# Attention and two expert blocks: the second block's table of rows kept in SBUF, and VectorE's operations in the attention in another order

## The chip, the core and the metric

The kernel runs on one NeuronCore of a Trainium2 chip. The core has TensorE (PE, matrix products), VectorE (DVE), ScalarE (ACT), GpSimd (POOL) and SyncE (SP, which here only issues transfers), and 16 DMA engines between DRAM and the on-chip memory SBUF; products land in the banks of PSUM. Each engine works through its own instructions in the order in which they are written. The metric is the device time of one execution in microseconds, and the numbers compared are medians of several runs.

## What is computed

Linear attention over 8 batches, 8 heads and 576 rows, then two blocks of experts over the 4608 rows with 8 experts each, of which every row uses one. The features of the attention are exponentials of a projection:

```python
def phi(x):
    proj = np.einsum('bhsd,df->bhsf', x, w_phi)
    proj = proj - np.max(np.abs(proj), axis=-1, keepdims=True)
    return np.concatenate([np.exp(proj), np.exp(-proj)], axis=-1)
q_p, k_p = (phi(q), phi(k))
kv = np.einsum('bhsf,bhsd->bhfd', k_p, v)
z = np.sum(k_p, axis=2)
num = np.einsum('bhsf,bhfd->bhsd', q_p, kv)
den = np.einsum('bhsf,bhf->bhs', q_p, z)[..., None] + 1e-06
return num / den

# a block: the expert of a row is the argmax of its logits
e_idx = np.argmax(logits, axis=1)
for e in range(E):
    mask = e_idx == e
    h = np.maximum(x[mask] @ w1[e], 0.0)
    out[mask] = gate_w[mask, None] * (h @ w2[e])   # block 2: also * sigmoid(x @ w_output_gate)[mask, e]
```

## The kernel before

**Products in halves.** Values in float32 are split into a high and a low float16 part, and three products stand for one (lines 878 to 880, 900 to 902). So every operand is scaled by a power of two and split first: `x_scale`, `x_hi` (ScalarE) and `x_lo` (VectorE) for the rows of the attention, `y_max`, `y_scale`, `y_hi`, `y_lo` for those of block 1.

**The attention** (to about 570 us) is a loop over steps t, nine for each batch, t = 9b + s. A step handles a pair of heads in several stages of a pipeline that lie some steps apart: projection of the keys and queries, then on VectorE the maxima `km` and `nm` and the difference `kd` (`k_max`, `q_max`, `k_sub`); five steps later the products `num` on TensorE, one more step later the division (`num_out` calls `norm`: `den`, its reciprocal, `xt`). A finished batch has its rows scaled and split (`x_hi` and `x_lo` at lag 16: 16 steps after the row's own), transposed on TensorE (`a_T`, lag 17, which reads both halves in the tile `rows_f`), and their logits are formed (`x_logits`, lag 18). In the steps with s = 1 the loop writes `a_T` ahead of `num`, in all others behind it.

**The splitter** (`Splitter.matrix`) prepares the weights of both blocks beside all this. For each expert and each of its two matrices (w = 0 and 1) it loads four quarters (`load`, two steps ahead), takes each quarter's largest magnitude (`mx`: on VectorE for w = 0; for w = 1 on ScalarE, whose line 247 writes `junk` and keeps the maximum), joins the four (`wm`, line 251, VectorE, and an all-reduce on GpSimd), and then forms `hi` on ScalarE and `lo` on VectorE and stores both to DRAM. Block 1's own steps do this for block 2's weights, in half-tile steps.

**The blocks.** A block goes through tiles of 128 rows, each of one expert: 40 main tiles and `E` = 3 more whose expert is found on the chip. Rows are gathered by an index (`gather`, an indirect DMA on GpSimd's queue), transposed (line 440 of `transposes`), and pass two products with a relu between (`first`, `hidden`, `second`); the relu's high half is written by ScalarE (line 889) and its low half by VectorE (line 890, tile `qs`). Rows that leave block 1 are scaled, split, transposed and given their logits of block 2; for each group of G = 4 tiles `gates` forms gates and one-hot choices, `gates_ranks` counts by products, `gates_store` stores the rows to `x2_d` and enters them in the table of block 2.

**The table.** Block 2 must know which stored row stands in which place of which expert. `places` works out a place for each of a group's rows. For the groups 0 to 8 of block 1, `enter` then writes the row's number (4 bytes) at that place: one indirect DMA (a scatter of 128 elements, line 434) for each of the group's four tiles, into four tables in DRAM that the attention had zeroed (`zeros`). The last group, and all of block 1's own table, go another way: `hots` writes two one-hot matrices for each tile on VectorE (lines 405 and 407, 128 x 128 with a code in place of the one, and 128 x 288), `tab_add` multiplies them in 12 products (line 416) into a bank of PSUM, and the result is added to a table of 96 x 384 in SBUF (`tab_out`), from which `tab_pick` reads by products and `decode` recovers the numbers. `route_a` and `route_b` form the indices of block 2 between the blocks: for block 2 from all four tables, read back from DRAM, and from the last group's.

The order of work on every engine is the order in which the functions are called. Short chains of VectorE operations are woven in by `Weave.step`, one operation at each `yield`.

```python
def enter(n, pi, c, r):
    nc.gpsimd.indirect_dma_start(
        out=tab_d[n][c][:, :], out_offset=bass.IndirectOffsetOnAxis(ap=pi[:, c : c + 1], axis=0),
        in_=row_no[n][:, r : r + 1], in_offset=None, bounds_check=NROW - 1, oob_is_err=False)
```

Of the kernel before, what the change touches and what calls it, by code (L numbers as in the profile page):

```python
# [26 lines left out]
DM = H * D  # L27
# [8 lines left out]
BIG = 8192.0  # L36
FAR = 65536.0
G = 4
# [16 lines left out]
def attention_two_moe(  # L55
# [15 lines left out]


    tab_d = [[dpool.tile([NROW, 1], F32, name=f"tab{n}_{k}") for k in range(K)] for n, K in enumerate((0, G))]
# [39 lines left out]
    row_no = [None]  # L113
    for n in (1,):
        nc_ = rows_of[n] // 128
        cn = const.tile([128, nc_], F32, name=f"cn{n}")
        nc.gpsimd.iota(cn, [[1, nc_]], base=-nc_, channel_multiplier=0, allow_small_or_imprecise_dtypes=True)
        t = const.tile([128, nc_, 2], F16, name=f"row_no{n}")
        nc.vector.tensor_copy(t[:, :, 0], cn)
        nc.vector.tensor_copy(t[:, :, 1], iota_p.to_broadcast([128, nc_]))  # L120
        row_no.append(t.rearrange("p c t -> p (c t)").bitcast(F32))


    tab0 = const.tile([96, 3, 128], F16, name="tab0")
    nc.gpsimd.memset(tab0, 0.0)
    code = const.tile([128, 5, 8], F32, name="code")
    nc.gpsimd.iota(code, [[0, 5], [-128, 8]], base=2047, channel_multiplier=-1, allow_small_or_imprecise_dtypes=True)
    for g in range(4):
        nc.vector.tensor_scalar(code[:, g], code[:, g], float(1 << (4 - g)), None, op0=ALU.mult)
    code = code.rearrange("p g c -> p (g c)")  # L130

    code1 = const.tile([128, G], F32, name="code1")
    nc.gpsimd.iota(
        code1, [[-128, G]], base=2047 - 128 * ((NMAIN - G) % 8), channel_multiplier=-1,
        allow_small_or_imprecise_dtypes=True)
    nc.vector.tensor_scalar(code1, code1, float(1 << (5 - (NMAIN - G) // 8)), None, op0=ALU.mult)
# [77 lines left out]
    class Splitter:  # L214
# [11 lines left out]
        def matrix(self, t0, e, w, stage):  # L226
# [12 lines left out]
            def mx(i):  # L239
# [9 lines left out]
                if i == 3:  # L249
                    m1 = self.sm.tile([128, 1], F32, tag="wm1", name="wm1")  # L250
                    nc.vector.tensor_reduce(out=m1, in_=st["mx"], op=ALU.max, axis=AX.X)
                    st["ma"] = self.sm.tile([128, 1], F32, tag="wma", name="wma")
                    nc.gpsimd.partition_all_reduce(st["ma"], m1, 128, RMAX)
# [113 lines left out]
    def places(ps, oh16, C, n, valid=None, chip=False):  # L367
# [19 lines left out]
        if n == 1 and not chip:  # L387
            return pi
# [10 lines left out]
    def hots(at_, pk, po, codes, mems):  # L399
# [3 lines left out]
        for c, m in enumerate(mems):  # L403
            a, o = m[:, 0:128], m[:, 128:416]
            nc.vector.tensor_scalar(
                a, iota128, pk[:, c : c + 1], codes[:, c : c + 1], op0=ALU.is_equal, op1=ALU.mult)
# [13 lines left out]
    def tab_out(ps):  # L420
        nc.vector.tensor_tensor(tab0, tab0, ps[0:96], op=ALU.add)

    def decode(out_, ps, tag, w, n=0):
# [4 lines left out]
        nc.vector.tensor_scalar(bits, bits, -1.0, float((137 << 10) + (5119, 6143)[n]), op0=ALU.mult, op1=ALU.add)  # L428
# [3 lines left out]

    def enter(n, pi, c, r):
        nc.gpsimd.indirect_dma_start(
            out=tab_d[n][c][:, :], out_offset=bass.IndirectOffsetOnAxis(ap=pi[:, c : c + 1], axis=0),
            in_=row_no[n][:, r : r + 1], in_offset=None, bounds_check=NROW - 1, oob_is_err=False)
# [68 lines left out]
    def zeros(z):  # L505

        nc.gpsimd.memset(z, 0.0)
        big = z[0:1, NROW // 128 :]
        nc.gpsimd.memset(big, BIG)
        yield  # L510
        for n in range(2):
            for t in tab_d[n]:
                nc.sync.dma_start(out=t.rearrange("(p c) o -> p (c o)", p=128), in_=z[:, 0 : NROW // 128])
                yield
        w = XW // 2
# [71 lines left out]
    etab = [None, const.tile([128, len(tab_d[1]), E], F32, name="etab1")]  # L587
# [38 lines left out]
    def early_rows(n):  # L626

        ereg[n] = [
            nc.values_load(eni[n][0:1, i : i + 1], engines=(ET.SP,), min_val=0, max_val=NE - 1) for i in range(2)]
        for k, t in enumerate(tab_d[n]):  # L630
            nc.sync.dma_start(
                out=etab[n][:, k],
                in_=t.rearrange("(e r) o -> e (r o)", e=NE)[ds(ereg[n][0], 1), 0 : E * 128].rearrange(
                    "e (c p) -> p (e c)", p=128))

    def early_sel():
# [4 lines left out]
            out=ec, in0=eno[0][:, 0:1].to_broadcast([128, E]), scalar=float(C1), in1=ec, op0=ALU.mult, op1=ALU.add)  # L641
# [6 lines left out]
    def tab_pick(ps, sel, tab=tab0):  # L648
        for k in range(3):
            nc.tensor.matmul(ps, tab[:, k], sel[:, k], start=(k == 0), stop=(k == 2))  # L650

    def early_idx(n, ps=None):
        if n == 0:
            yield from decode(eidx[0], ps, "ebits", E)
        else:
# [1330 lines left out]
```

## Time and profile before

| | before |
|---|---|
| Median of three runs | 1509.79 us (1503.33, 1509.79, 1510.79) |
| Profiled execution | 1502.37 us, its span 1500.5 us |
| Busy in the span: TensorE, VectorE, ScalarE, GpSimd | 1401.5, 824.6, 649.0, 198.7 us |
| Granted clock of TensorE, mean | 0.962 of full speed |
| DMA | 286.50 MB in 162224 packets, 191 GB/s in the mean |

The stages in the profiled execution: attention to about 521 us, its last rows and the turn to block 1 to 572, block 1 to 1064, the turn to block 2 to 1100, then block 2. Windows are stretches of the span; a row has each engine's busy time with the number of its instructions. In a timeline row stand the start, the duration in us, engine, line, operation, what it writes and reads, shapes, and in brackets the idle time ahead of it with what ended it; "issue" there means that the engine waited for nothing that the profile shows. In a row of waits stand the engine and line that waited, what released it, us in total, times, and the longest. The queue q8 carries instructions, q1 the transfers that SyncE issues, q0 those of GpSimd.

### The profile page before, as it was taken

The numbers are of one execution on the slowest core, as the hardware profiler recorded it, in microseconds if no ns is written. First come the engines' busy times: TensorE is split into PE (matmuls) and PEld (weight loads), VectorE is DVE, ScalarE is ACT, GpSimd is POOL, SyncE is SP. The second block draws the span as 40 slices with busy tenths as digits, with TensorE's granted clock in tenths as the row PEclk, the third lists the DMA queues.
The fourth block names the chain that finished last, engine by engine and source line by source line (L and its number), as shares of the span: only waits on it lengthen the run. The fifth ranks groups of instructions, "written<-read, shape, count | busy, mean of one in ns | idle before, by whom it ended". The sixth has DMA issues, their size and how long they took to land. (4 is left out here: it accounts for less than half of the span.)

```text
span 1500.5 us, 39967 instructions
## 1 busy us (share of the span) xinstructions
PE 1401.5 (93%) x16045; PEld 1134.8 (76%) x16045; DVE 824.6 (55%) x2469; ACT 649.0 (43%) x1010; POOL 198.7 (13%) x244
## 2 busy tenths in 40 slices
PE   6999999989989989999999789889999999999997
PEld 4998888988889877767777567667677777777764
DVE  3677887887887767667777467555621111111110
ACT  1457566766758432555556346443211111111111
POOL 1000000000000001212221121122022121121211
PEclk8999999999999889999999899999999999999998
DMA  8377858768663544578878788789835262773470
GB/s 242 112 208 233 257 169 259 217 233 249 201 199 114 210 191 130 191 191 226 220 218 258 147 181 242 157 229 358 241 110 155 72 191 65 240 229 93 130 239 30
DMA packets 162224, 286.50 MB, mean 191 GB/s; under 512 B 88537, under 2 KB 91117, under 8 KB 154864
## 3 DMA queue, kind: packets, MB, share of 16 engines
q1 hardware_dynamic: 146496, 242.29, 54.7%
q0 software_dynamic: 13504, 41.42, 8.5%
q8 instruction: 129, 2.11, 0.6%
q14 instruction: 63, 0.52, 0.1%
q10 hardware_dynamic: 2032, 0.16, 0.1%
HBM read 444.63 MB, written 99.24 MB: 362 GB/s over the span
## 5 line engine op out<-in xcount | busy, mean ns | idle before, releaser
L890 DVE SCALAR_TENSOR_TENSOR qs<-proj,qs 128x512 f16<-128x512 f32 x107 | 73.6, 688 | 270.8 <-ACT qs L889 270.8
L1497 PE MATMUL num<-kvsb,E 128*128 128x65 f32 x1024 | 128.4, 280 | 28.7 <-DVE xt L1481 27.0
L878 PE MATMUL proj<-xT,w 128*128 128x128 f16 x896 | 153.2, 220 | 1.3 <-DMA xT<-xg 0.7
L880 PE MATMUL proj<-xT,w 128*128 128x128 f16 x896 | 153.1, 220 | 0.1
L879 PE MATMUL proj<-xT,w 128*128 128x128 f16 x896 | 153.2, 220 | 0.0
L1497 PEld LDWEIGHTS num<-kvsb,E 128*128 128x128 f32 x1024 | 123.4, 197 | 33.5 <-issue 23.7
L880 PE MATMUL proj<-xT,v 128*128 128x128 f16 x816 | 140.5, 220 | 4.9 <-issue 4.9
L878 PE MATMUL proj<-xT,v 128*128 128x128 f16 x816 | 140.5, 220 | 0.0
L879 PE MATMUL proj<-xT,v 128*128 128x128 f16 x816 | 140.4, 220 | 0.0
L889 ACT ACTIVATE qs<-proj 128x512 f16<-128x512 f32 x107 | 63.5, 593 | 173.9 <-PE proj L880 142.9
L878 PEld LDWEIGHTS <-w 128*128 128x128 f16 x1344 | 132.3, 98 | 7.1 <-issue 5.0
L879 PEld LDWEIGHTS <-w 128*128 128x128 f16 x1344 | 132.3, 98 | 4.1 <-issue 2.1
L1412 PE MATMUL kv<-v,kp 128*128 128x128 f32 x1024 | 135.2, 288 | 0.0
L880 PEld LDWEIGHTS <-w 128*128 128x128 f16 x1344 | 132.3, 98 | 0.7 <-issue 0.6
L900 PE MATMUL num<-w,qs 128*128 128x512 f16 x336 | 127.3, 379 | 0.6 <-DMA w<-pl 0.6
L902 PE MATMUL num<-w,qs 128*128 128x512 f16 x336 | 127.3, 379 | 0.0
L901 PE MATMUL num<-w,qs 128*128 128x512 f16 x336 | 127.3, 379 | 0.0
L1412 PEld LDWEIGHTS kv<-v,kp 128*128 128x128 f32 x1024 | 126.4, 201 | 0.4 <-issue 0.4
L878 PEld LDWEIGHTS <-v 128*128 128x128 f16 x1216 | 120.0, 99 | 7.9 <-issue 5.7
L901 PE MATMUL num<-ks,qs 128*128 128x512 f16 x304 | 116.5, 383 | 9.2 <-issue 9.1
L902 PE MATMUL num<-ks,qs 128*128 128x512 f16 x304 | 116.6, 384 | 6.9 <-issue 6.9
L901 PEld LDWEIGHTS <-qs 128*128 128x128 f16 x640 | 62.9, 98 | 78.3 <-issue 13.1
(371 smaller groups left out, 3626.6 us busy)
## 6 DMA issues: line engine op xcount, KB each, us to landing
w<-pl SPq DMA_DIRECT2D x152, 1024.0 KB
v<-pl SPq DMA_DIRECT2D x80, 1024.0 KB
ks<-pl SPq DMA_DIRECT2D x80, 1024.0 KB
pl<-wo SPq DMA_DIRECT2D x66, 512.0 KB
w<-in_moe_w_dram SPq DMA_DIRECT2D x64, 512.0 KB
wf<-in_moe_w_dram SPq DMA_DIRECT2D x64, 512.0 KB
pl<-qs SPq DMA_DIRECT2D x26, 512.0 KB
ks<-in_k_dram SPq DMA_DIRECT2D x16, 576.0 KB
```

Of the source, the lines that this page charges most:

```text
L878: nc.tensor.matmul(h[:, j], wk[:, 0, cs], xT[:, k], start=(k == 0), stop=False)
L879: nc.tensor.matmul(h[:, j], wk[:, 0, cs], xT[:, 4 + k], start=False, stop=False)
L880: nc.tensor.matmul(h[:, j], wk[:, 1, cs], xT[:, k], start=False, stop=(k == 3))
L889: nc.scalar.activation(out=hi, in_=h, func=AF.Relu)
L890: nc.vector.scalar_tensor_tensor(out=lo, in0=h, scalar=0.0, in1=hi, op0=ALU.max, op1=ALU.subtract)
L900: nc.tensor.matmul(y, h[:, 0, k], wk[:, 0], start=(k == 0), stop=False)
L901: nc.tensor.matmul(y, h[:, 0, k], wk[:, 1], start=False, stop=False)
L902: nc.tensor.matmul(y, h[:, 1, k], wk[:, 0], start=False, stop=(k == 7))
L1412: nc.tensor.matmul(ps[:, half, h % 2], kp[:, c, half, :], vw(v1, 4 * h + c), start=(h % 2 == 0 and half == 0 and c == 0), stop=False)
L1497: nc.tensor.matmul(ps[:, c, 0:V], e[:, half, 128 * c : 128 * c + 128], kw(g, half), start=(half == 0), stop=(half == 1))
```

## The change

All ten groups of block 1 are entered by products into a second table in SBUF, `tabs[1]`. The scatters, their four tables in DRAM, the zeroing of these and both reads of them are gone; `hots` now runs for every group, and `enter_rows` issues the 12 products between `first` and `hidden` of the next tile. `early_idx` and `route_b` read the table by three products and `decode`, for both blocks alike.

In the attention three things change places. `norm` runs its first two operations (`den` and reciprocal) ahead of `k_max`, so that `xt` follows `km` directly and stands ahead of `nm`. `x_lo` has lag 17 instead of 16 and stands right behind the end of `norm`, so in the step of its row's `a_T`. In the splitter the maximum on ScalarE comes one step (in block 1 one half-tile step) earlier, while `wm` and the all-reduce, now in `most`, stay where they were.

```diff
@@ in Splitter.matrix
-                if i == 3:
-                    m1 = self.sm.tile([128, 1], F32, tag="wm1", name="wm1")
...
+                if i == 3 and w == 0:
+                    most()
+
+            def most():
+                m1 = self.sm.tile([128, 1], F32, tag="wm1", name="wm1")
...
-                job(u, "mx", mx, i)
+                job(u - w, "mx", mx, i)
...
+            if w == 1:
+                job(t0 + 3 * gap, "mx", most)
@@ the table
-    def tab_out(ps):
-        nc.vector.tensor_tensor(tab0, tab0, ps[0:96], op=ALU.add)
+    def tab_out(n, ps):
+        nc.vector.tensor_tensor(tabs[n], tabs[n], ps[0:96], op=ALU.add)
...
-    def enter(n, pi, c, r):
-        nc.gpsimd.indirect_dma_start(
...
@@ in early_rows and route_a: the reads of the tables in DRAM
-        for k, t in enumerate(tab_d[n]):
-            nc.sync.dma_start(
-                out=etab[n][:, k],
...
-            nc.sync.dma_start(out=tab, in_=t.rearrange("(k c p) o -> c k (p o)", k=3, p=128))
@@ in route_b
-            for x in range(2):
-                for i, t in enumerate(tab16):
-                    for k in range(3):
-                        nc.tensor.matmul(
-                            rows[:, x], t[:, k, :, x], sel[:, k], start=(i == 0 and k == 0),
-                            stop=(i == len(tab16) - 1 and k == 2))
-            last = state["pg"][:, 3, 2 * M : 3 * M]
-            tab_pick(last, sel, state["tab1"])
...
+        tab_pick(n, state["pg"][:, 3, 0:M], sel)
+        done(decode(idx, state["pg"][:, 3, 0:M], "bits", M, n))
@@ in gates_store
-        pi = yield from places(gate.pop((j, "rk")), gate.pop(j), g_, 1, val2[:, i0 : i0 + g_])
-        for c in range(g_):
-            enter(1, pi, c, i0 + c)
+        pk, po = yield from places(gate.pop((j, "rk")), gate.pop(j), g_, 1, val2[:, i0 : i0 + g_])
+        at_ = []
+        yield from hots(
+            at_, pk, po, codes[1][:, i0:],
+            [state["late"].tile([128, 416], F16, tag="hot", name="hot", bufs=G) for _ in range(g_)])
+        state["hots"] = at_[0]
...
+    def enter_rows():
+
+        if "hots" in state:
+            state["pts"] += 1
+            tab_out(1, tab_add(state["pt"][state["pts"] % len(state["pt"])], state.pop("hots")))
@@ in the blocks' loop
                 first(*nxt_, 0)
-            if "hots1" in state:
-                last_rows()
+            enter_rows()
             if nxt_:
                 hidden(*nxt_, 0)
@@ in the attention's loop
             norm_ = num_out(*at(6)) if at(6) else iter(())
+            next(norm_, None)
             next(norm_, None)
...
             done(norm_)
+            if at(17, 0) and at(17)[0] < B - 1:
+                x_lo(*at(17))
             each(6, x_max)
...
-            if at(16, 0) and at(16)[0] < B - 1:
-                x_lo(*at(16))
```

GpSimd in block 1, around a group's scatters; `xg` are the gathered rows of a tile, `x_d` the stored rows, `tab_0` to `tab_3` the tables. Before:

```order
L1015 DMA x_d<-qs_151 128x4x520
L848 DMA xg_146<-x_d,idx_6996 128x520
L434 DMA tab_0_64<-row_no_100,pi 36864x1
L434 DMA tab_1_65<-row_no_100,pi 36864x1
L434 DMA tab_2_66<-row_no_100,pi 36864x1
L434 DMA tab_3_67<-row_no_100,pi 36864x1
L848 DMA xg_147<-x_d,idx_6996 128x520
L253 ISA wma<-wm_8341 128x1
```

And now:

```order
L955 DMA x_d<-qs_146 128x4x520
L788 DMA xg_141<-x_d,idx_6988 128x520
L788 DMA xg_142<-x_d,idx_6988 128x520
L242 ISA wma<-wm_8350 128x1
L788 DMA xg_142<-x_d,idx_6988 128x520
```

The four scatters are gone, and the gather of the next tile follows the one ahead of them.

VectorE in block 1, at the end of a group's `places`; `pi`, `pk` and `po` are the group's places, the rows with `wf` belong to the splitter, `mx` is the maximum of a tile's rows of block 1. Before:

```order
L385 CAST pi<-po 128x4
L243 TENSOR_REDUCE wmx<-wf_6798 128x1
L974 TENSOR_TENSOR c_9075<-qs_151,wgi 128x1
L976 TENSOR_SCALAR lg<-qf,c_9075 128x16
L890 SCALAR_TENSOR_TENSOR qs_152<-proj,qs_152 128x512
L978 SCALAR_TENSOR_TENSOR lg<-qf,c_9075,lg 128x16
L269 SCALAR_TENSOR_TENSOR qs_150<-wf_6799,sb,qs_150 128x2x512
L930 TENSOR_TENSOR c<-xg_147,fac_7006 128x1
L932 TENSOR_REDUCE mx<-num 128x1
```

And now, where only the first of four pairs that write `hot` stands:

```order
L379 TENSOR_SCALAR pi<-pi 128x4
L382 CAST pk<-pi 128x4
L830 SCALAR_TENSOR_TENSOR qs_147<-proj,qs_147 128x512
L384 TENSOR_TENSOR po<-po,pk 128x4
L258 SCALAR_TENSOR_TENSOR qs_145<-wf_6791,sb,qs_145 128x2x512
L394 TENSOR_SCALAR hot<-iota_78,pk,code_102 128x128
L396 TENSOR_SCALAR hot<-iota_c,po 128x288
...
L870 TENSOR_TENSOR c<-xg_142,fac_6998 128x1
L872 TENSOR_REDUCE mx<-num 128x1
L877 TENSOR_TENSOR mx<-mx,c 128x1
```

Three small operations on the places and eight that write `hot` have come in ahead of `c` and `mx`.

VectorE in an attention step with s = 1; `rows_f` is written by `x_lo`, and the rows with `w_` belong to the splitter. Before, from `den` on, where the `rows_f` at the end is for the `a_T` of the next step:

```order
L1477 TENSOR_SCALAR den<-num 128x4
L1383 TENSOR_REDUCE km<-proj 128x4
L1479 RECIPROCAL den<-den 128x4
L1340 TENSOR_REDUCE nm<-proj 128x4
L1481 TENSOR_TENSOR xt<-num,den 128x4x64
L1389 TENSOR_TENSOR kd<-proj,km 128x512
L204 TENSOR_SCALAR pb<-wma 128x1
L206 TENSOR_SCALAR pb<-pb 128x1
L209 TENSOR_SCALAR sb<-pb 128x1
L210 TENSOR_SCALAR winv<-pb 128x1
L1584 SCALAR_TENSOR_TENSOR rows_f<-xt,sb,rows_f 128x512
L269 SCALAR_TENSOR_TENSOR xT_149<-w_1_160,sb,xT_149 128x2x512
```

And now, where the `rows_f` is for the `a_T` of the same step:

```order
L1413 TENSOR_SCALAR den<-num 128x4
L1415 RECIPROCAL den<-den 128x4
L1319 TENSOR_REDUCE km<-proj 128x4
L1417 TENSOR_TENSOR xt<-num,den 128x4x64
L1276 TENSOR_REDUCE nm<-proj 128x4
L1325 TENSOR_TENSOR kd<-proj,km 128x512
L190 TENSOR_SCALAR pb<-wma 128x1
L1520 SCALAR_TENSOR_TENSOR rows_f<-xt,sb,rows_f 128x512
L192 TENSOR_SCALAR pb<-pb 128x1
L195 TENSOR_SCALAR sb<-pb 128x1
L196 TENSOR_SCALAR winv<-pb 128x1
```

`xt` stands ahead of `nm`, and `x_lo`'s write of `rows_f` ahead of the rest of the splitter's scale.

## Rows read from the trace of the kernel before

**Rows 1.** Windows: span and busy us per engine, granted clock, DMA share, GB/s.
```profile
390.00:521.00 131.00, 121.47 (x1330) 115.03 (x1329) 102.43 (x294) 87.37 (x146) 4.19 (x6) 0.96 0.53 176
...
572.00:809.24 237.24, 234.32 (x2908) 176.69 (x2906) 169.34 (x547) 128.47 (x181) 47.48 (x50) 1.00 0.72 201
809.24:1064.63 255.39, 228.12 (x2717) 169.26 (x2715) 147.80 (x520) 113.42 (x158) 48.85 (x51) 0.94 0.82 219
1064.63:1100.00 35.37, 30.99 (x324) 21.34 (x322) 20.98 (x88) 5.88 (x10) 8.81 (x9) 0.95 0.67 222
```

**Rows 2.** TensorE's waits, 809.24 to 1064.63: us in total, times, longest.
```profile
PE num L901 <- issue: 8.4, 1, 8.4
PE num L902 <- issue: 5.8, 2, 5.0
PE proj L880 <- issue: 4.9, 1, 4.9
```

**Rows 3.** Windows behind the four long waits, and their sum.
```profile
842.50:847.50 5.00, 4.14 (x10) 1.53 (x11) 1.95 (x3) 2.42 (x3) 0.00 (x0) 0.50 0.82 253
...
sum 17.10, PE 14.45 PEld 8.95 DVE 5.32 ACT 7.94 POOL 0.30; mean PE 3.61 PEld 2.24 DVE 1.33 ACT 1.99 POOL 0.07
```

**Rows 4.** Timeline of GpSimd, its first scatter before the first long wait.
```profile
823.64 1.03 POOL L434 DMA_INDIRECT tab<-row_no,pi  x1 [0.30 <-issue]
```

**Rows 5.** Tile `tab`: count, ns minimum, median, maximum, first and last start.
```profile
L434 POOL DMA_INDIRECT tab<-row_no,pi x36: 977/994/1757, 633.8 to 1046.4; - x36
...
L421 DVE TENSOR_TENSOR tab<-tab,px x6: 540/542/546, 190.5 to 504.2; 96x384 f16<-96x384 f16 x6
```

**Rows 6.** Windows at and after that group of scatters.
```profile
822.00:828.00 6.00, 6.00 (x47) 3.17 (x45) 4.37 (x10) 2.92 (x4) 4.81 (x4) 1.00 0.85 301
828.00:842.00 14.00, 6.16 (x108) 5.83 (x105) 6.38 (x18) 2.21 (x3) 2.42 (x4) 0.83 0.84 43
```

**Rows 7.** Page, DMA queues over the span: packets, MB, share of the engines.
```profile
q8 instruction: 129, 2.11, 0.6%
```

**Rows 8.** DMA queues from 828 to 843, columns as before.
```profile
q1 hardware_dynamic: 319, 0.72, 82.9%
```

**Rows 9.** TensorE's waits in the attention, 76 to 521.
```profile
PE num L1497 <- DVE xt L1481: 26.2, 22, 2.5
```

**Rows 10.** VectorE's waits in the attention, 76 to 521.
```profile
DVE wm L251 <- ACT junk L247: 20.7, 7, 5.3
```

**Rows 11.** Line 440, transposes leaving block 1 in two undisturbed groups.
```profile
L440 PE MATMUL px<-ident,rw x5: 219/219/219, 715.8 to 716.0; 128*128 128x128 f16 x5
...
L440 PE MATMUL px<-ident,qs x6: 219/219/219, 762.4 to 762.7; 128*128 128x128 f16 x6
```

**Rows 12.** Timeline of TensorE in an attention step with `s == 1`.
```profile
333.03 0.61 PE L440 MATMUL px<-ident,rows_f 128*128 128x128 f16 x8
334.21 0.55 PE L1497 MATMUL num<-kvsb,E 128*128 128x65 f32 x3 [0.57 <-DVE xt L1481]
```

**Rows 13.** Line 416 by form, the last group's products.
```profile
L416 PE MATMUL pl<-hot x12: 219/219/257, 1078.0 to 1079.1; 128*96 128x128 f16 x12
```

**Rows 14.** VectorE's groups by line, 1075 to 1081.2: busy us, mean ns.
```profile
L407 DVE TENSOR_SCALAR hot<-iota_c,po 128x288 f16<-128x288 f16 x4 | 1.3, 327 | 0.0
```

**Rows 15.** Timeline of VectorE in block 1, beside a group of scatters.
```profile
637.63 0.69 DVE L932 TENSOR_REDUCE mx<-num 128x1 f32<-128x512 f32 x1 [1.58 <-issue]
```

**Rows 16.** Timeline of VectorE in the attention step of rows 12.
```profile
333.16 0.66 DVE L1340 TENSOR_REDUCE nm<-proj 128x4 f32<-128x512 f32 x1
...
334.07 0.68 DVE L1389 TENSOR_TENSOR kd<-proj,km 128x512 f32<-128x512 f32 x1
...
336.58 0.75 DVE L1584 SCALAR_TENSOR_TENSOR rows_f<-xt,sb,rows_f 128x512 f16<-128x512 f32 x1 [0.51 <-ACT rows_f L1579]
```

**Rows 17.** Timeline of SyncE's queue, a load of weights for `junk`.
```profile
687.30 0.40 SPq L236 DMA_DIRECT2D wf<-in_moe_w_dram  x1
```

**Rows 18.** Timeline of ScalarE shortly after that load's issue.
```profile
690.86 1.15 ACT L260 ACTIVATE wo<-wf,sb 128x1024 f16<-128x1024 f32 x1
```

More of the change, by code (lines that the diff above doesn't have):

```diff
@@ L111, in attention_two_moe @@
     nc.gpsimd.iota(col_no, [[96, 3]], base=1, channel_multiplier=1, allow_small_or_imprecise_dtypes=True)
[L113 to L136, printed above, removed]
+    tabs = [const.tile([96, 3, 128], F16, name="tab0")]
+    nc.gpsimd.memset(tabs[0], 0.0)
+    codes = []
+    for n in range(2):
+        c = const.tile([128, 5 + n, 8], F32, name=f"code{n}")
+        nc.gpsimd.iota(
+            c, [[0, 5 + n], [-128, 8]], base=2047, channel_multiplier=-1, allow_small_or_imprecise_dtypes=True)
+        for g in range(4 + n):
+            nc.vector.tensor_scalar(c[:, g], c[:, g], float(1 << (4 + n - g)), None, op0=ALU.mult)
+        codes.append(c.rearrange("p g c -> p (g c)"))
     iota_c = const.tile([128, NROW // 128], F16, name="iota_c")
@@ L505, in zeros @@
     def zeros(z):
+        w = XW // 2
         nc.gpsimd.memset(z, 0.0)
-        big = z[0:1, NROW // 128 :]
+        big = z[0:1, w : w + 1]
         nc.gpsimd.memset(big, BIG)
         yield
[L511 to L515, printed above, removed]
         for c in range(NMAIN, NSLOT):
@@ L1023, in gates_store @@
         later = j == NMAIN // G - 2
-        if not rush and not later:
-            rows_store(j)
-        if rush:
-            rows_store(j, DM)
-            pk, po = yield from places(gate.pop((j, "rk")), gate.pop(j), g_, 1, val2[:, i0 : i0 + g_], True)
-            at_ = []
-            yield from hots(
-                at_, pk, po, code1, [state["late"].tile([128, 416], F16, tag="hot", name="hot", bufs=G) for _ in range(G)])
-            state["hots1"] = at_[0]
-            return
-        pi = yield from places(gate.pop((j, "rk")), gate.pop(j), g_, 1, val2[:, i0 : i0 + g_])
-        for c in range(g_):
-            enter(1, pi, c, i0 + c)
+        if not later:
+            rows_store(j, DM if rush else 0)
+        pk, po = yield from places(gate.pop((j, "rk")), gate.pop(j), g_, 1, val2[:, i0 : i0 + g_])
[4 more added lines that the diff above has]
+        state["hots"] = at_[0]
         if later:
             rows_store(j)
-    def last_rows():
-        state["pts"] += 1
-        ps = tab_add(state["pt"][state["pts"] % len(state["pt"])], state.pop("hots1"))
-        state["tab1"] = state["late"].tile([96, 3, 128], F16, name="chip1")
-        nc.vector.tensor_copy(state["tab1"], ps[0:96])
+    def enter_rows():
+        if "hots" in state:
+            state["pts"] += 1
+            tab_out(1, tab_add(state["pt"][state["pts"] % len(state["pt"])], state.pop("hots")))
     def run(seq):
@@ L1661, in x_hots @@
             pk, po = rows.pop((b, "pk"))
-            yield from hots(at_, pk, po, code[:, 9 * (b // 2) + 4 * (b % 2) :], mems)
+            yield from hots(at_, pk, po, codes[0][:, 9 * (b // 2) + 4 * (b % 2) :], mems)
             rows[b, "hots"] = at_[0]
@@ L1887, in attention_two_moe @@
         x_enter(last - 1)
[L1888 removed]
+        tab_out(0, rows.pop((last - 1, "pt")))
         tiles()
@@ L1902, in attention_two_moe @@
     rwb.append(late.tile([128, G, XW], F32, name="rw1"))
+    tabs.append(late.tile([96, 3, 128], F16, name="tab1"))
+    nc.gpsimd.memset(tabs[1], 0.0)
     nc.gpsimd.memset(rwb[1][:, :, DM:XW], 0.0)
```

83 lines of the change are left out of this document (26 added, 57 removed).

## The prediction

> **What bounds the kernel now.** I began with the table of windows, which cuts the span into stages [rows 1]. In the first block of experts (572 to 1064 us) TensorE is busy nearly always: 234.32 of 237.24 us at full clock up to 809, then 228.12 of 255.39 us at clock 0.94. So TensorE is the bound there, and the second half loses what the first does not: 27.3 us idle and a lower clock, for nearly the same products. The waits of TensorE name the loss [rows 2]: four single waits of 8.4, 5.0, 4.9 and (not among the rows) 4.7 us, released by "issue", that is, by nothing that the profile shows on another engine. After each of them TensorE runs for 4 to 5 us at clock 0.50, its lower level of 1.2 GHz [rows 3].
>
> What is late there? The first of the four ends at 842.5, and 19 us ahead of that GpSimd issues the first of four scatters of 128 four-byte elements into the tables in DRAM [rows 4], one group of nine [rows 5]. Up to 828 the DMA queues move 301 GB/s; in the 14 us after, they show a share of 0.84 and move 43 GB/s: packets are open but don't land [rows 6]. The code of TensorE comes by such packets too: the page counts 129 on the instruction queue, 2.11 MB, so 16.4 KB each and one in some 12 us of the span [rows 7]. In the queue table for 828 to 843, queue q8 is not listed, and q1 alone takes 82.9% of the engines' time [rows 8]. That fits an engine that has run out of instructions: it waits for "issue" until a packet of code lands. The same collapse follows every one of the nine groups of scatters and occurs nowhere else; only when TensorE's code is due within it does the engine stop. That the scatters cause it is my reading; the trace shows the order in time only.
>
> In a sentence apart: the Trainium skill, "DMA: Bandwidth & Descriptors", section Specifications, says that transfers under 512 B are done as read-modify-write, which would make 4-byte writes dear; the trace agrees in so far as the slow stretch starts with them.
>
> In the attention (76 to 521) the bound is shared: TensorE is busy 121.47 of 131 us and VectorE 102.43 in the row of 390 to 521 [rows 1], and the two wait for others in turn: TensorE's products `num` wait for VectorE's `xt` 22 times, 26.2 us [rows 9], and VectorE waits for ScalarE's `junk` 7 times, 20.7 us [rows 10].
>
> **Part 1, the scatters go.** They are 36 indirect DMAs. What goes with them, if my reading holds, is the idle time of TensorE in block 1, 2.92 + 27.27 = 30.2 us [rows 1], and half of the 14.45 us of work at half clock, summed over the four stretches [rows 3], 7.2 us: 37.4 us. At least the four long waits and the clock go, 23.0 + 7.2 = 30.2 us. A second way: the transposes of the rows that leave block 1 come once per four tiles, at 715.8 and 762.4 [rows 11], so an undisturbed tile takes 46.6 / 4 = 11.65 us; 39 tiles are 454.4 us, and the two windows together hold 492.6, which is 38.2 more. **I take 37, between 30 and 38.**
>
> **Part 2, the products that take their place.** Nine more groups make 12 products each on TensorE. Such products stand 0.056 us apart (eight of 128x128 take 0.61 us and one alone 0.22, so (0.61 - 0.22) / 7 [rows 12]), so 0.67 us a group, 6 us in all, and in full on the path, since TensorE is the bound. The one group that the kernel before does so took from 1078.0 to 1079.3 with its waits [rows 13]; nine times 1.3 is 12. **I take 6, between 6 and 12.**
>
> On VectorE each group adds three small operations, eight that write `hot`, and one add into the table. The larger form of `hot` takes 0.33 us [rows 14], so eight take 2.6 us at most. They stand ahead of `mx`, before which VectorE sits idle for 1.58 us in that step [rows 15]: `mx` is at most 1.0 us later. TensorE itself arrives 0.67 us later by the products, so at most 0.4 us a group remain, 3 us in nine. The add stands ahead of the lower half of a relu (`qs`); the same add takes 0.54 us in the attention [rows 5], which uncovered costs 5 us in nine groups. VectorE is busy only 147.80 of 255.39 us there [rows 1]. **I take 0 for all of it, between 0 and 8.**
>
> **Part 3, the turn to block 2** (1064 to 1100). TensorE is idle for 4.4 of 35.4 us, and clock 0.95 says that about a tenth of the stretch ran at the lower level, which costs 1.8 us [rows 1]. 24 of its 27 table products, four loads of tables and three VectorE operations go. **I take 3 us of gain, between 0 and 6.** The zeroing of the tables was hidden under the attention, and I cost it at nothing.
>
> **Part 4, the attention.** Here the change is an exchange of places, and I see gains and one loss.
>
> The gain: `xt` moves ahead of one reduction (`nm`, 0.66 us [rows 16]). All 22 waits of TensorE for `xt` have a mean of 1.2 us, so each can shrink by 0.66: 14.5 us. ScalarE's `junk` one step earlier lets VectorE's waits for it go, 20.7 us, but these are mostly VectorE's and end in slack; I give them 1 us of TensorE. With a few smaller waits beside the 26.2 us, 15.5 is about a half of what TensorE waits here. Clock 0.96 in 390 to 521 is about 10.5 us at the lower level, which costs 5.2 in 131 us [rows 1], so some 18 in the 445 us of the attention; as at block 1, such stretches follow waits, and I let a half go with them: 8.5. Gain 24.
>
> The loss: in the second step of a batch (`s == 1`) TensorE does `a_T`, the transposes of `rows_f`, ahead of `num`. Before, `x_lo`, which writes the second half of `rows_f`, was done in the step ahead. Now it is done in the same step, behind `km`, `xt`, `nm` and `kd`. At 333.03 the eight transposes start at once, and `num` follows at 334.21 [rows 12]. `kd` starts at 334.07 and runs 0.68 us; `x_lo` takes 0.75 [rows 16]. So `x_lo` would end at about 335.4, and the transposes would start 2.4 us later than at 333.03; of `num`'s 1.8 us of delay I let about 1.1 be taken up by the wait of the next step, which leaves 0.7. Waits of more than a microsecond were followed by half clock, and 3.4 us of it cost 1.7. That is 2.4 us in each of six batches: 14 us. It can be 0 (VectorE early by as much), or 6 x (1.8 + 1.7) = 21.
>
> **Attention net: 10 us of gain, between 24 of gain and 14 of loss.**
>
> ScalarE's `junk` is also earlier in block 1. There it reads a load that was issued at 687.3 [rows 17]; now it stands right behind the ScalarE operation that starts at 690.86 and takes 1.15 us [rows 18], so the load has 4.7 us. If loads land as fast as the undisturbed stretch lets them, this costs little; I take 0, and the case in which it does not is a rival.
>
> **The sum.** The profiled run took 1502.4 us, 1.9 beyond its span. 1502.4 - 37 + 6 + 0 - 3 - 10 = 1458.4. The median of the runs is 7.4 us above the profiled run and the lowest run 1.0; I add half of the 7.4, which gives **1462 us**.
>
> **The rivals.** *The fetch is late for another reason (A).* If packets of code are held up by the ordinary loads, the 37 us stay: 1462 + 37 = 1499. For it: the four waits lie in the second half alone, although scatters run from 633.8 on [rows 5]. Against it: the loads are the same in the first half, and 43 GB/s isn't a queue that is full of loads. In a sentence apart: the Trainium skill, "DMA: Bandwidth & Descriptors", section Queues, rings and completion order, says that each engine goes round its queues packet by packet, by which a packet of code would not wait long behind other queues; the row of 82.9% for q1 alone can't decide it. Chance 0.08, half of it under the bound of 0.5%.
>
> *The attention loses (B).* The transposes wait at `s == 1` and the swap of `xt` brings nothing, because `xt` waits for the same thing as `km`: 14 of loss in place of 10 of gain, 1462 + 24 = 1486. For it: VectorE is busy 78% of the time [rows 1], so little can move `x_lo` forward. Against it: 22 waits for `xt`. Chance 0.18.
>
> *ScalarE stalls in block 1 (C, the slower side).* If loads go on to take 14 us, as in the slow stretch [rows 6], `junk` waits 14 - 4.7 = 9.3 us with the relus of block 1 queued behind it on ScalarE, and TensorE waits for those: in seven experts 65 us, 1527. It decides from (1517 - 1462) / 7 = 7.9 us a wait on, so if loads land later than 12.6 us after issue. It needs slow transfers without scatters. Chance 0.04.
>
> **How the numbers follow.** My forecast has a chance of 0.70. B is inside the range's upper end, the attention's full gain with a little of Part 3 makes its lower end: 1442 to 1486. About 0.5% (7.5 us) is what a measurement of this kernel can tell from no change. Faster by more: 0.70 + 0.18 + half of A = 0.92; slower by more: C with most of its chance, 0.03; the rest, 0.05, is the same.
>
> **What would show it.** Right: block 1 shows no "issue" wait of over 2 us on TensorE, clock 1.00 throughout, DMA rows of over 150 GB/s after each group, and transposes 47.3 us apart all through; at `s == 1` a wait of `px` for `x_lo`'s `rows_f` of some 2 us in six batches; waits of `num` for `xt` under 15 us. Wrong: "issue" waits that stay (A), waits of ScalarE's `junk` for `wf` in block 1 (C), or `xt` waits as long as before (B). My weakest term is the attention's, a difference of two numbers of about 24 and 14.

## The result and the profile after

The changed kernel takes 1468.28 us (median of four runs, 1466.54 to 1473.65) against 1506.56 us before: a ratio of 0.9752, interval 0.9709 to 0.9794. The prediction said 1462, between 1442 and 1486. The profiled execution took 1468.27 us with a span of 1466.4, so 34.1 us of span are gone. Block 1 gave about what the sum had put there; the attention, which was to give 10 us, gave none.

The windows of the kernel after, in the stages of [rows 1] (span, then busy us of TensorE, its weight loads, VectorE, ScalarE and GpSimd, then TensorE's granted clock, DMA share, GB/s). The stages are the attention, the turn to block 1, block 1 from the first to the last transposes of its rows, the turn to block 2, and block 2:

```profile
76.00:521.00 445.00, 418.17 (x4572) 396.01 (x4569) 362.17 (x940) 290.98 (x482) 13.13 (x15) 0.92 0.66 210
521.00:578.50 57.50, 50.78 (x601) 45.17 (x600) 34.86 (x136) 17.65 (x30) 4.11 (x8) 0.79 0.47 186
578.50:1037.40 458.90, 458.68 (x5732) 348.01 (x5730) 339.31 (x1172) 242.37 (x338) 54.08 (x65) 1.00 0.68 231
1037.40:1067.50 30.10, 26.85 (x262) 16.99 (x259) 19.32 (x84) 5.89 (x10) 6.80 (x8) 1.00 0.38 136
1067.50:1466.40 398.90, 390.92 (x4448) 285.64 (x4448) 56.66 (x150) 69.60 (x111) 73.91 (x72) 0.99 0.48 144
```

And the same marks in the kernel before:

```profile
76.00:521.00 445.00, 411.72 (x4614) 389.75 (x4611) 358.81 (x945) 294.10 (x488) 12.55 (x17) 0.95 0.66 211
521.00:572.30 51.30, 45.24 (x564) 39.88 (x564) 32.71 (x130) 15.41 (x26) 1.88 (x6) 0.83 0.54 215
572.30:1064.90 492.60, 462.42 (x5621) 345.92 (x5619) 317.11 (x1062) 241.89 (x338) 96.32 (x101) 0.97 0.78 211
1064.90:1096.60 31.70, 27.38 (x287) 17.73 (x284) 20.02 (x87) 5.88 (x10) 7.10 (x8) 1.00 0.68 226
...
1096.60:1500.50 403.90, 392.63 (x4448) 287.28 (x4448) 56.67 (x149) 69.60 (x111) 73.52 (x72) 0.99 0.48 142
```

Block 1 went from 492.6 to 458.9 us, 33.7 less, and holds no idle time of TensorE to speak of (0.2 us) at full clock. The turn to block 2 gave 1.6, and block 2 with the end 5.0. Up to the start of block 1 the kernel is **6.2 us later**. In the same 445 us TensorE was idle for 26.8 us instead of 33.3, but its clock fell from 0.95 to 0.92. One mark for the end of the attention is the table pick, the three products that read block 1's own table (line and operation, ns minimum, median, maximum, first and last start; the kernel before, then after):

```profile
L650 PE MATMUL pl<-esel,tab x3: 164/166/169, 517.1 to 517.2; 96*128 96x3 f16 x3
```

```profile
L624 PE MATMUL pl<-esel,tab x3: 164/164/169, 519.8 to 519.8; 96*128 96x3 f16 x3
```

It comes 2.7 us later. The turn to block 1 behind it takes 3.5 us longer (58.8 us at a mean clock of 0.80, where the kernel before has 55.3 at 0.85: some 7 us more at half speed, which accounts for it). The pick moves by some 5 us between kernels whose attention is written alike (513.7 to 518.5 us in five of those below), and e3 below, with the same three changes in the attention, has it at 513.5. So 2.7 us alone prove little.

In block 1 the only wait of TensorE left, where the kernel before had four long ones (three of them are in [rows 2]), is this:

```profile
PE px L424 <- DMA xg<-x_d,idx: 0.2, 1, 0.2
```

The transposes that leave block 1, line 424 now, four tiles apart as in [rows 11]:

```profile
L424 PE MATMUL pl<-ident,rw x8: 219/219/219, 744.3 to 744.7; 128*128 128x128 f16 x8
```

```profile
L424 PE MATMUL px<-ident,qs x8: 219/219/219, 791.6 to 792.0; 128*128 128x128 f16 x8
```

47.3 us lie between them, 0.7 more than the 46.6 of the kernel before: the 12 products. VectorE in the same kind of step as in [rows 15], with the last of the eight `hot` writes:

```profile
643.40 0.29 DVE L396 TENSOR_SCALAR hot<-iota_c,po 128x288 f16<-128x288 f16 x1
643.60 0.15 DVE L870 TENSOR_TENSOR c<-xg,fac 128x1 f32<-128x1 f32 x1
643.67 0.69 DVE L872 TENSOR_REDUCE mx<-num 128x1 f32<-128x512 f32 x1
```

The idle 1.58 us ahead of `mx` are filled, and TensorE does not wait behind it. And the 14 us after a group of rows is entered, beside the 43 GB/s of [rows 6]:

```profile
833.00:847.00 14.00, 14.00 (x193) 11.17 (x189) 11.08 (x37) 5.86 (x9) 1.38 (x2) 1.00 0.57 176
```

In the attention, TensorE's waits from 76 to 521 of the kernel after:

```profile
PE num L1433 <- DVE xt L1417: 9.6, 12, 1.7
PE px L424 <- DVE rows_f L1520: 7.6, 4, 2.2
PE px L405 <- DVE wo L396: 4.5, 18, 0.4
PE px L424 <- DVE pb L192: 4.1, 2, 2.0
```

The waits for `xt` fell from 26.2 us [rows 9] to 9.6. The two rows of `px L424` are new: six waits of 2 us, 11.7 in all, in the step s = 1. There the transposes `a_T` of a finished row stand ahead of `num`. One of them in the timelines of TensorE and VectorE, the step of [rows 12, 16]:

```profile
327.85 0.38 PE L424 MATMUL px<-ident,rows_f 128*128 128x128 f16 x4
330.22 0.40 PE L424 MATMUL px<-ident,rows_f 128*128 128x128 f16 x4 [1.99 <-DVE rows_f L1520]
330.45 2.33 PE L1433 MATMUL num<-kvsb,E 128*128 128x65 f32 x16
```

```profile
327.89 0.41 DVE L1417 TENSOR_TENSOR xt<-num,den 128x256 f32<-128x256 f32 x1
...
328.82 0.68 DVE L1325 TENSOR_TENSOR kd<-proj,km 128x512 f32<-128x512 f32 x1
329.42 0.74 DVE L1520 SCALAR_TENSOR_TENSOR rows_f<-xt,sb,rows_f 128x512 f16<-128x512 f32 x1
```

The four transposes of the high halves run, the four of the low halves wait until `x_lo` (line 1520) is through, and `num` waits behind them in TensorE's queue, though the `xt` of this step is done at 328.30. What follows shows in the windows of the kernel after around this wait:

```profile
332.30:335.80 3.50, 3.50 (x27) 3.14 (x27) 1.76 (x6) 2.30 (x4) 0.63 (x1) 0.50 0.48 123
328.00:331.00 3.00, 1.01 (x13) 0.84 (x12) 3.00 (x5) 2.39 (x5) 0.00 (x0) 1.00 0.92 264
335.80:340.00 4.20, 4.20 (x27) 4.20 (x27) 4.13 (x10) 2.53 (x5) 0.00 (x0) 0.66 0.37 149
```

After the wait comes a stretch of 3.5 us at clock 0.50, its lower level of 1.2 GHz, and another 4.2 us at 0.66, of which some 2.9 are at the lower level: 6.4 us at half clock cost 3.2, more than the wait itself. Not every such wait is followed by half clock: behind the one of 2.05 us that ends at 138.05 the clock stays at 1.00 from 139 to 165.

### The profile page after: what moved, and what is told of

It is laid out like the page before. It is cut to its first block, busy times and chain, and to the rows that moved or that the text cites. A ratio compares the mean times of both kernels' runs of the same rounds, so it can differ in the third digit from the quotient of the medians.

```text
span 1466.4 us, 40153 instructions
## 1 busy us (share of the span) xinstructions
PE 1407.8 (96%) x16132; PEld 1146.3 (78%) x16132; DVE 852.2 (58%) x2579; ACT 649.7 (44%) x1010; POOL 159.4 (11%) x208
## 5 line engine op out<-in xcount | busy, mean ns | idle before, releaser
L819 PE MATMUL proj<-xT,v 128*128 128x128 f16 x816 | 138.7, 219 | 0.1
L820 PE MATMUL proj<-xT,v 128*128 128x128 f16 x816 | 138.7, 219 | 0.0
L818 PE MATMUL proj<-xT,v 128*128 128x128 f16 x816 | 138.7, 219 | 0.0
L1348 PE MATMUL kv<-v,kp 128*128 128x128 f32 x1024 | 138.4, 292 | 0.0
L1433 PEld LDWEIGHTS num<-kvsb,E 128*128 128x128 f32 x1024 | 126.4, 201 | 13.1 <-issue 7.8
L1348 PEld LDWEIGHTS kv<-v,kp 128*128 128x128 f32 x1024 | 129.5, 205 | 0.4 <-issue 0.4
L819 PEld LDWEIGHTS <-v 128*128 128x128 f16 x1216 | 118.9, 98 | 2.5 <-issue 0.3
L818 PEld LDWEIGHTS <-v 128*128 128x128 f16 x1216 | 118.9, 98 | 2.1
L820 PEld LDWEIGHTS <-v 128*128 128x128 f16 x1216 | 118.9, 98 | 0.0
```

Source lines behind the costliest of these rows:

```text
L818: nc.tensor.matmul(h[:, j], wk[:, 0, cs], xT[:, k], start=(k == 0), stop=False)
L819: nc.tensor.matmul(h[:, j], wk[:, 0, cs], xT[:, 4 + k], start=False, stop=False)
L820: nc.tensor.matmul(h[:, j], wk[:, 1, cs], xT[:, k], start=False, stop=(k == 3))
L1348: nc.tensor.matmul(ps[:, half, h % 2], kp[:, c, half, :], vw(v1, 4 * h + c), start=(h % 2 == 0 and half == 0 and c == 0), stop=False)
L1433: nc.tensor.matmul(ps[:, c, 0:V], e[:, half, 128 * c : 128 * c + 128], kw(g, half), start=(half == 0), stop=(half == 1))
```

## The experiments

All ratios are to the kernel before in the same set of runs. The table has each kernel's median, its ratio with the interval, the start of the table pick, and the time of block 1 between its first and last transposes. The pick and block 1 are from the profiled execution. The sets differ a little: the median of the kernel before lies at 1506.56 us in the set of the kernel after, at 1509.89 in that of e2, e3, e4 and e7, at 1510.13 in that of t4, t4_apart, t512 and e9, at 1511.49 in that of e8, e10 and e11, and at 1515.34 in that of t4_64. So a few microseconds between rows of different sets mean little.

| kernel | us | ratio (95%) | pick at | block 1 |
|---|---|---|---|---|
| before | 1506.56 | 1 | 517.1 | 492.6 |
| after | 1468.28 | 0.9752 (0.9709 to 0.9794) | 519.8 | 458.9 |
| e2 table only | 1461.15 | 0.9683 (0.9648 to 0.9719) | 513.7 | 458.8 |
| e3 attention only | 1527.43 | 1.0122 (1.0087 to 1.0157) | 513.5 | 517.3 |
| e4 after, num first | 1433.70 | 0.9493 (0.9460 to 0.9525) | 492.2 | 458.8 |
| e7 after, x_lo back | 1446.77 | 0.9583 (0.9547 to 0.9620) | 502.7 | 458.8 |
| e8 table only, num first | 1462.98 | 0.9686 (0.9648 to 0.9724) | 520.6 | 458.8 |
| e9 x_lo back, num first | 1441.04 | 0.9560 (0.9513 to 0.9607) | 499.0 | 458.8 |
| e10 e4, junk back | 1453.51 | 0.9618 (0.9578 to 0.9657) | 510.0 | 458.8 |
| e11 e4, norm back | 1448.68 | 0.9573 (0.9536 to 0.9611) | 506.7 | 458.8 |
| t4 e2 and scatters of 4 B | 1497.12 | 0.9914 (0.9886 to 0.9942) | 516.8 | 495.5 |
| t4_64 the same, 64 B apart | 1465.73 | 0.9689 (0.9620 to 0.9757) | 518.5 | 458.9 |
| t4_apart the same, 512 B apart | 1466.59 | 0.9709 (0.9668 to 0.9750) | 518.4 | 459.0 |
| t512 e2 and scatters of 512 B | 1463.67 | 0.9689 (0.9646 to 0.9733) | 518.1 | 458.9 |

### Which part brings the gain: e2 and e3

e2 is the changed kernel with these undone:

```diff
-            next(norm_, None)
...
             done(norm_)
-            if at(17, 0) and at(17)[0] < B - 1:
-                x_lo(*at(17))
...
+            if at(16, 0) and at(16)[0] < B - 1:
+                x_lo(*at(16))
...
-                job(u - w, "mx", mx, i)
+                job(u, "mx", mx, i)
```

> The changed kernel with the three changes in the attention and the splitter undone, so the kernel before with all groups of block 1 entered by products. Theory: the whole gain comes from block 1, where no scatter leaves the DMA queues slow; block 1's 39 tiles take 457 to 462 us (492.6 before), no wait of TensorE for 'issue' of over 2 us there, and the attention is as before (its table pick at 517 us); time 1458 to 1466 us where the changed kernel takes 1468. Rival, that the changes in the attention carry some 10 us of the gain: 1474 to 1482.

Measured: 1461.15 us, ratio 0.9683. Block 1 holds most of the gain (33.8 of 44.0 us of span; another 7 lie behind it), and the attention's changes as made don't add to it: the kernel after is some 7 us slower than e2, with intervals that overlap a little, so a small loss or none.

e3 is the kernel before with those three changes and nothing else.

> The kernel before with only the three changes in the attention and the splitter. Theory: TensorE's transposes at s = 1 wait some 2 us for x_lo in each of six batches and half clock follows, which eats what the shorter waits for xt bring; the attention's table pick comes at 518 to 522 us instead of 517, block 1 keeps its 'issue' waits (485 to 500 us for 39 tiles); time within 0.5% of the kernel before, 1500 to 1513 us. Rival, the prediction's own net of 10 us of gain: 1490 to 1497.

Measured: 1527.43 us, slower than the kernel before by 1.2%, which neither theory had. The attention is not to blame (its pick is at 513.5, earlier than the 518 to 522 expected). Block 1 is: 517.3 us. The waits of ScalarE and then of TensorE in its block 1:

```profile
ACT junk L247 <- DMA wf<-in_moe_w_dram: 64.1, 11, 10.8
```

```profile
PE qf L450 <- ACT xT L967: 16.8, 6, 5.5
PE pl L445 <- DMA xg<-x_d,idx: 10.5, 3, 6.7
```

ScalarE waits 64.1 us for the loads that `junk` reads, TensorE waits behind it for tiles that ScalarE should have copied. This is the mechanism of the prediction's rival C, which had 65 us of such waits, in a kernel where transfers are slow: it keeps the scatters, and `junk` stands half a tile earlier. But C let all 65 us reach the total, and here block 1 is only 24.7 us longer than before. TensorE's waits for "issue" have shrunk to 4.6 us in it, so the one delay took in part the other's place; that the total came out at C's 1527 is chance. In the changed kernel the scatters are gone, and `junk` has no row among ScalarE's waits in block 1. So the two halves of the change aren't independent: of the three changes only the earlier `junk` touches block 1, and it costs 25 us there with the scatters and nothing without them (458.9 us after, 458.8 in e2).

### Are the scatters the cause: t4, t4_apart, t512, t4_64

These four start from e2 and put 36 indirect DMAs back into GpSimd's queue, into tables in DRAM that nothing reads. What is shown is t4; t4_apart multiplies the places by 128 and t4_64 by 16, with tables and bound as much longer, and t512 has rows of 128 elements:

```diff
         nc.vector.tensor_copy(pi, po)
         yield
+        if n == 1 and not rush:
+            pe = sp.tile([128, CM], I32, tag="pe", name="pe")[:, 0:C]
+            nc.vector.tensor_scalar(pe, po, 1.0, None, op0=ALU.mult)
+            for c in range(C):
+                nc.gpsimd.indirect_dma_start(
+                    out=scr_d[c][:, :], out_offset=bass.IndirectOffsetOnAxis(ap=pe[:, c : c + 1], axis=0),
+                    in_=fill, in_offset=None, bounds_check=NROW * 1 - 1, oob_is_err=False)
```

> The kernel e2_table_only (table by products, attention as before) with the 36 scatters of 4 bytes put back, at the same places in GpSimd's queue and with the same indices, into tables in DRAM that nothing reads. Theory, that the scatters by themselves slow the DMA queues and with them the fetch of TensorE's code: block 1's 39 tiles go from 458.8 back to 480 to 505 us, with 'issue' waits of 3 to 9 us and half clock after them, and 20 to 70 GB/s for some 10 us after each group. Rival, that the reads and the zeroing of the tables or the ordinary loads were to blame: 458 to 464 us.

> As t4, but each 4-byte element lands 512 bytes from its neighbour (indices times 128, tables 128 times as long), where in t4 neighbours in place are 4 bytes apart. If what is slow is many small writes into the same few bytes of DRAM, block 1 stays at 458 to 466 us; if any write of 4 bytes is as dear, or the indirect DMA itself, it comes to 480 to 505 us as in t4.

> As t4, with elements of 512 bytes (128 times the data, 64 KB in each scatter). If the cost lies in writes of less than 512 bytes, block 1 stays at 458 to 466 us and the queues move over 150 GB/s after each group; if the cost is that of an indirect DMA of 128 elements whatever its size, 480 to 505 us.

> As t4_apart, but neighbours in place land 64 bytes apart instead of 512 (indices times 16). t4 showed the slow queues (block 1 495 us), t4_apart none (458.8). If what collides are small writes into the same 64 bytes or less, block 1 stays at 458 to 462 us; if they collide within some hundred bytes, it lies at 475 to 500 us.

Measured, the windows of the 14 us after the group near 826 us and of block 1, first t4:

```profile
831.70:845.70 14.00, 11.38 (x117) 7.61 (x115) 8.13 (x22) 4.63 (x6) 1.42 (x3) 0.88 0.88 81
571.80:1067.30 495.50, 470.83 (x5736) 353.99 (x5734) 342.48 (x1186) 241.04 (x338) 94.52 (x102) 0.98 0.79 210
```

t4_apart, then t4_64, then t512:

```profile
830.20:844.20 14.00, 14.00 (x190) 11.17 (x188) 11.28 (x36) 6.48 (x8) 1.43 (x3) 1.00 0.62 198
```

```profile
830.00:844.00 14.00, 14.00 (x190) 11.17 (x188) 11.29 (x36) 6.48 (x8) 1.43 (x3) 1.00 0.63 199
```

```profile
829.60:843.60 14.00, 14.00 (x190) 11.17 (x188) 11.26 (x36) 6.52 (x8) 1.41 (x2) 1.00 0.61 203
```

With the scatters of 4 bytes back, block 1 is back at 495.5 us, 36.7 above e2, with the slow queues (81 GB/s at a share of 0.88, somewhat above the 20 to 70 expected) and TensorE's waits for "issue". The three costliest rows of these in t4's block 1:

```profile
PE qf L437 <- issue: 5.8, 1, 5.8
PE num L847 <- issue: 3.2, 2, 2.5
PE pl L429 <- issue: 2.6, 2, 2.2
```

Nothing reads these tables and nothing zeroes them, so the scatters alone do it. And it is neither the count of indirect DMAs nor the size of an element: the same 36 with 4 bytes each, 64 or 512 bytes apart, cost nothing that can be seen, and 512 bytes each cost nothing either. What is dear is that neighbours in the table, which are neighbours in place within an expert, lie 4 bytes apart. One thing is not separated: with 64 or 512 bytes between places all elements also begin at the same offset within 64 bytes, and no run spreads them by an uneven step.

Why TensorE waits for "issue" stays open. The prediction read it as waiting until a packet of code lands. In the kernel before queue q8 shows no packet from 824 to 845, where [rows 7] has one in some 12 us, which fits. But the longest wait ends at 842.53:

```profile
842.53 0.59 PE L901 MATMUL num<-ks,qs 128*128 128x512 f16 x1 [8.37 <-issue]
```

That is before the next packet of q8, which runs between 845 and 847. The waits that end at 898.15 and 1003.78 are alike: no packet of q8 from 885.2 to 901.5, and none from 992.5 to 1010. The page's other instruction queue, q14, shows none within these three waits either. So the rows show slow queues and a late engine, and the landing of a packet, as the queue records it, did not end these three waits. No run made the code's packets late by themselves.

### Where the attention loses: e4, e7, e8, e9

e4 is the changed kernel with `num` ahead of `a_T` in every step:

```diff
-            if s != 1:
-                each(5, num)
+            each(5, num)
             if at(18, 0) and at(18)[0] < B - 1:
                 x_logits(*at(18))
             if at(17, 0) and at(17)[0] < B - 1:
                 a_T(*at(17))
-            if s == 1:
-                each(5, num)
```

> The changed kernel, but at s = 1 TensorE does num ahead of the transposes a_T, as in all other steps. Theory: the transposes' waits for x_lo (11.7 us with those put down to the splitter's pb) fall below 5 us, the half clock behind them goes, the attention's granted clock comes back from 0.92 to 0.95 or more, and its table pick comes 8 to 18 us earlier than at 519.8; time 1450 to 1461 us. Rival, that the wait goes elsewhere (num waits for its own operands, or the transposes are late for the next user of their bank): 1464 to 1472.

Measured: 1433.70 us, below the whole range, and the fastest of all the kernels here: its ratio is 0.949 where the changed kernel's is 0.975. TensorE's waits for `rows_f` are gone from the table of waits. The windows of 76 to 490, first of the kernel after, then of e4:

```profile
76.00:490.00 414.00, 388.71 (x4316) 368.30 (x4313) 339.87 (x852) 276.60 (x458) 13.13 (x15) 0.93 0.66 210
```

```profile
76.00:490.00 414.00, 395.77 (x4524) 375.29 (x4521) 359.38 (x933) 288.50 (x480) 13.15 (x15) 0.97 0.69 220
```

Of the 27.6 us by which the pick is earlier, 7.1 are idle time of TensorE that is gone. The clock's step from 0.93 to 0.97 means that about 33 us less (twice 0.04 of 414) ran at half speed, which is worth 17. So six waits of 2 us cost less by themselves than by the clock behind them. The rest of the 34.6 us between the profiles (1468.27 and 1433.65) is the turn to block 1, which takes 52.1 us from the pick on in e4, at a clock of 0.90, where the kernel after takes 58.7.

e7 is the changed kernel with `x_lo` back at lag 16 and its old place, e9 is e7 with `num` first, e8 is e2 with `num` first.

> The changed kernel with x_lo back at lag 16 and at its old place; xt ahead of nm and the earlier junk stay. Theory: no transposes wait for x_lo at s = 1; the waits for xt stay short; VectorE waits again for ScalarE's x_hi (some 10 to 20 us in the attention), which costs TensorE only a part. Table pick 5 to 12 us earlier than at 519.8; time 1456 to 1464 us. Rival, that x_lo's waits at lag 16 held TensorE as much as the new wait does: 1466 to 1471.

> The kernel e2_table_only with num ahead of the transposes at s = 1 and nothing else of the attention changed. If the order num first is worth something by itself, the table pick comes 3 us or more ahead of e2's 513.8 and the time is 1450 to 1458 us; if it is only worth what x_lo's wait cost, 1458 to 1466.

> The kernel e7_xlo_back (x_lo at lag 16 as before) with num ahead of the transposes at s = 1 too. If the order num first gains by itself, because num's wait for xt there shrinks or TensorE has work while it waits, it comes below e7's 1446.8, near e4's 1433.7; if num first was only worth what x_lo's wait cost, it stays at 1442 to 1450.

Measured: e7 1446.77 us, faster than expected; the pick is 17 us earlier than in the changed kernel. e8 1462.98 us, so `num` first is worth nothing in the attention as it was: e2 takes 1461.15, and the intervals lie over one another (its pick, at 520.6, is 6.9 us later than e2's). e9 1441.04 us, between its two cases: some 6 below e7, with intervals that overlap widely, and 7 above e4, where they overlap a little; its pick is 6.8 us later than in e4. So moving `x_lo` to the step of its transposes is a loss of some 22 us (1468.28 against 1446.77) if `num` stands behind them, and a gain of some 7 if it stands ahead, the latter barely clear of noise.

### What the other two moves are worth: e10 and e11

e10 is e4 with the splitter's `junk` at its old step, e11 is e4 with `xt` behind `nm` again.

> The kernel e4_num_first with ScalarE's junk back at its old step. The prediction gave the earlier junk 1 us of TensorE's time, by which this takes 1433 to 1438 us; if VectorE's 20.7 us of waits for junk reach TensorE, with the half clock behind them, 1440 to 1450.

> The kernel e4_num_first with the division in its old order (xt behind nm). The prediction gave the exchange 14.5 us of shorter waits for xt and most of the clock's 8.5: 1446 to 1457 us, waits for xt back at 20 to 27 us; if other work fills in for it, 1434 to 1441.

Measured: e10 1453.51 us, e11 1448.68. Beside the other moves the earlier `junk` is worth 20 us, more than either theory had, and the exchange of `xt` and `nm` 15 (12 by the ratios). TensorE's and VectorE's waits in e10 from 76 to 490, then TensorE's in e11:

```profile
PE num L1428 <- DVE xt L1412: 20.6, 18, 3.1
```

```profile
DVE wm L237 <- ACT junk L233: 19.5, 7, 5.1
```

```profile
PE num L1433 <- DVE xt L1417: 20.2, 17, 2.4
```

In e4 the same waits for `xt` are 13.2 us. The waits of VectorE for `junk` don't all end in slack: behind the one of 3.69 us that ends at 137.43 in e10, TensorE waits 3.10 us for the next `xt`; behind the one of 5.13 us that ends at 471.61, only 0.73. The single effects (20, 15 and 7) add up to more than the 29 us between e8 and e4, so they overlap: each is measured with the others in place.

## Why the prediction was right, and where it was not

The total held: 1468.28 in 1442 to 1486, 6 us above the likeliest value, and clearly faster. By its steps:

**Parts 1 and 2, the scatters and the products.** Forecast -37 + 6 = -31; block 1 gave -33.7. The products cost 0.7 us a group, as worked out, and VectorE's additions are hidden in full. The reading behind it, that the scatters slow the queues, which the trace before showed only as an order in time, is shown by t4. The link behind it, that TensorE stops until a packet of code lands, is not: three of the four waits end without one. Rival A (the fetch is late for another reason) is out: no "issue" wait is left.

**Part 3, the turn to block 2.** Forecast -3, measured -1.6. Block 2 and the end, which the sum left at nothing, gave another 5.0.

**Part 4, the attention: the step that failed.** Forecast a net gain of 10. The kernel after takes 7 us more than e2, which has the same block 1 and the old attention; its pick is 2.7 us later than before, and the turn to block 1, for which the sum had no term, 3.5 longer. Both terms of the difference were mis-sized. The gain of 24: e7 has the exchange of `xt` and the earlier `junk` and leaves `x_lo` where it was, and it is 14.4 us faster than e2 (1446.77 against 1461.15). The loss of 14: moving `x_lo` from there costs 21.5 us (1468.28 against 1446.77; 17.1 at the pick), just above the top of the range given for it, 21. Its mechanism, place, count of six and wait (2.0 us, 2.4 forecast) were right, its price was not. The forecast had 1.7 us of clock in each batch, from one stretch of 3.4 us at half speed, and let the next step take up most of `num`'s delay; the step at 327 us was followed by 6.4 us at half speed, 3.2 of cost. The 24.9 us by which e4's pick is ahead of the kernel before are not a measure of the 24, though they look like one: `num` stands first in e4, and there the move of `x_lo` gains.

The split of the 24 was wrong as well: `junk` was given 1 us, and taking it back out of e4 costs 20; `xt` and its share of the clock were given most of the rest, and taking that out costs 12 to 15. That the total still came out is partly luck. Against the terms of the sum, block 1 gave 2.7 us more than forecast, the turn to block 2 1.4 less, block 2 with the end 5.0 that no term had, and the attention with the turn to block 1 was 16.2 worse (6.2 of loss for 10 of gain).

**Rival B**, the attention at +14, came nearer than the forecast in this one term: +2.7 at the pick and 6.2 by the start of block 1, for a different reason than it named (the waits for `xt` did shrink). **Rival C** is not in the changed kernel, and e3 shows its waits where scatters remain, at 25 us of block 1 in place of 65.

What carried the forecast through was that the block's term was large and rested on idle time that could be read off directly; the attention's was a difference of two terms of about its own size.

## What to carry to other kernels

A transfer that nothing waits for can still be the most expensive in a kernel: look at GB/s beside the DMA share in the microseconds after it. Spacing the entries by 64 bytes already made the scatters harmless in block 1 (t4_64); a kernel with such a spaced table in place of the products, which it would have to read back, was not run. When an operation is moved later, look in each order variant of the loop for the consumer that now stands right behind it on an in-order engine, and for what is queued behind that consumer; one exception for one step of nine cost more here than the move gained. Price a long wait of TensorE together with the half clock that follows it in the trace's own stretches (here up to 6.4 us of it behind a wait of 2) before weighing it against many short waits. And when two changes of order meet in one kernel, undo each by itself: what the pair gives doesn't tell what either is worth.

## What the runs showed of the hardware

**Small writes that lie close together.** Four scatters of 128 elements of 4 bytes each, into places 4 bytes apart, left the queues at 43 GB/s (81 in t4) for 14 us; the same elements 64 bytes apart left 199, 512 apart 198, and elements of 512 bytes 203. The Trainium skill, "DMA: Bandwidth & Descriptors", section Specifications, gives a smallest size of 512 B for full rate and read-modify-write below it. If that alone made them dear, t4_64 and t4_apart should have been as dear as t4; they were not, so here the size alone doesn't decide, and what does is how close the writes lie (or, as said, where in 64 bytes they begin). Whether the collision is in DRAM or in the engines' write path is not told by these runs.

**The end of the program.** From the end of the last indirect DMA of GpSimd to the end of the span the kernel before takes 9.2 us, the kernel after 5.8 (their last rows in GpSimd's timeline, before, then after, then t4_64):

```profile
1490.36 0.98 POOL L915 DMA_INDIRECT out_dram<-yo,ti  x1 [4.19 <-ACTq L1913]
```

```profile
1459.61 0.98 POOL L855 DMA_INDIRECT out_dram<-yo,ti  x1 [4.20 <-ACTq L1852]
```

```profile
1454.58 0.98 POOL L860 DMA_INDIRECT out_dram<-yo,ti  x1 [4.20 <-ACTq L1856]
```

t4_64, whose span is 1464.6 us, takes 9.0 again, although its scatters cost nothing where they run. e2, without them, takes 5.8. So some 3.4 of the 5.0 us in block 2 and its end go with having these 36 DMAs in the program; how is open.
